# Whole-array modulation, uneven VectorE exp copies, a ring of 24 and reciprocal DMAs queued late, in an attention and GEGLU block planned by its own time model

## The chip, the cores and the metric

One core of one Trainium2 chip. The time is the device time of one execution, in microseconds (us), as a median over runs. A single core's run counts as "fast" when it is within 1.5% of the fastest run of the same kernel, otherwise "slow". Engine names in the profile: PE is TensorE (PEld its weight loads), ACT is ScalarE, DVE is VectorE, POOL is GpSimd, SP is the engine that issues the DMAs.

## The reference

```python
mod = (silu(c) @ w_mod).reshape(1, 6, 1, 512)          # sa, ca, ga, sb, cb, gb
h = layernorm(x) * (1 + ca) + sa                       # x: 2048 tokens x 512
q, k, v = h @ wqkv                                     # 32 heads of 16
p = softmax(q @ k.T / 4)                               # 32 x 2048 x 2048 exps
x = x + ga * ((p @ v) @ wo)
h = layernorm(x) * (1 + cb) + sb
out = x + gb * ((gelu(h @ w_gate) * (h @ w_up)) @ w_down)   # hidden size 1792
```

The 134 million exps are most of the work of the busiest engine (ScalarE, 842 of 902 us below). Scores are made transposed, 128 keys by 512 queries of one head at a time, so there are 32 x 16 x 4 = 2048 score tiles of 128x512.

## The kernel before

The kernel is a planner in Python: it keeps a small time model of the engines, decides by it which instruction comes next, and emits five fixed instruction streams. Every change to it, to its model as well, changes the order of everything that follows.

A score tile goes one of two ways. ScalarE exponentiates two or three at once into slots of a ring E; TensorE's PV matmuls read them and so free the slots. Or VectorE makes a "quad": it evicts four tiles, one for each of four heads, writing a linear function of the score as the bits of a bf16 number, which is a rough power of two; it then makes four copies with a constant added to the bits, and PV adds all five. Before, each copy was weighed by a V scaled to match:

```python
SHIFT = (26, 51, 77, 102)
NSL = 12            # slots of the ring E (CH = 3 per exp)
T0 = 12             # only key tiles 12 to 15 may be quads
...
v = self.vs[:, i - 1, kt - T0, :] if i else self.vaug[:, kt, :]     # scaled V for copy i
...
cand = [k for k, (u, r, g0) in enumerate(rounds)
        if u not in units[:2] and r * (512 // u[3]) >= T0]
...
if len(mem) == CH and "modB" in self.have and self.free["dve"] < t + 700:    # start or go on with a quad
```

The modulation product is a run of one-column matmuls. The helper `mm` splits any matmul of 128 rows and 128 columns of weights into four pieces of 32 columns, unless `whole` is set:

```python
def mod_cols(self, bank, base):
    for ci in range(8):
        for dc in range(NDC):            # 4
            self.mm(bank[:, ci:ci + 1], self.wmod[:, dc, base + P * ci:base + P * ci + P],
                    self.sc_bf[:, dc:dc + 1], start=(dc == 0), stop=(dc == NDC - 1))
```

At the end of a unit (one group of four heads for one set of queries) the softmax sums travel through DRAM: out, back in as 128 rows, reciprocal, out, and back broadcast. The whole chain was put into SP's queue in order:

```python
self.dma("sp", s1..., self.osb[DH:P:32, lo:hi], ...)
self.dma("sp", den, s1..., ...)
def fin1():
    self.recip(rden, den)
    self.dma("sp", s2..., rden, ...)
    for j in range(4):
        self.dma("sp", self.rb[32 * j:32 * j + 32, lo:hi], s2...broadcast_to([32, W]), ...)
...
self.task([fin1], ("den", u))
```

There are 24 units of 512 queries, then 13 of 256 and 6 of 128; QKV projections run beside the first eight, the FFN of one set of queries beside the attention of the next.

The softmax here doesn't subtract the row's maximum and nothing guards it: scores larger than these inputs give would overflow.

## Time and profile before

| | before |
|---|---|
| median of the first runs | 901.15 us (900.17 to 903.19) |
| span of the profiled run | 902.3 us |
| ScalarE busy / not busy (gaps) | 842.0 us / 60.3 us |
| VectorE busy | 687.8 us |
| VectorE evictions for quads | 188 + 92 = 280 |
| first exp | 23.59 us |

Read it from ScalarE: the span is its busy time plus the time it is not busy, its gaps. A change helps by taking work off it or by closing its gaps. The profiled run is one of the slower ones: in the rounds of the experiments the kernel before has medians of 898 to 899 us, a span of some 897, so gaps read against 60.3 us look about 6 us better than they are. Stretches of the kernel before (us; PE, PEld, DVE, ACT, POOL busy us with counts; granted TensorE clock; DMA share; GB/s):

```profile
10.00:20.00 10.00, 4.51 (x102) 2.70 (x96) 2.58 (x8) 1.55 (x2) 0.00 (x0) 0.59 1.08 363
11.90:22.10 10.20, 6.08 (x58) 2.87 (x57) 3.49 (x9) 2.24 (x3) 0.00 (x0) 0.50 1.00 348
...
90.00:100.00 10.00, 8.65 (x190) 2.48 (x186) 3.86 (x8) 6.84 (x6) 0.00 (x0) 0.69 0.03 5
93.80:104.10 10.30, 9.46 (x63) 1.69 (x62) 5.28 (x9) 6.38 (x7) 0.00 (x0) 0.50 0.09 28
95.00:100.00 5.00, 5.00 (x34) 0.89 (x33) 2.23 (x4) 2.05 (x2) 0.00 (x0) 0.50 0.03 5
```

In this profile the clock is at one half from 11.9 us, which is 1.4 us into the wait that began at 10.53, and again from 93.8 us, after the second modulation burst; each time for 10.2 us. From 95 to 100 us TensorE is busy for all of 5.00 us with only 34 matmuls while ScalarE works 2.05.

### The profile page before, as it was taken

To read this page: it belongs to the slowest core of one execution; us is meant where nothing else is said; L and a number is where in the kernel's file an instruction comes from. 1 tells how busy PE (TensorE), PEld (TensorE's weight loads), DVE (VectorE), ACT (ScalarE), POOL (GpSimd) and SP (SyncE) were. 2 spreads that over 40 slices of the span, in tenths; PEclk is the share of its full clock that TensorE was granted. 3 is DMA by queue.
4 is the path that set the end of the run, shared out by engine and by line. 5 is a ranking of instruction groups with operands and counts; after the bars stand their busy time and mean duration, and the time that the engine had idled before them with its cause. 6 is when DMAs were issued, how large, how long until landed. Compare 5 with 4: busy or idle time off the path is not lost.

```text
span 902.3 us, 28354 instructions
## 1 busy us (share of the span) xinstructions
PE 820.0 (91%) x12817; PEld 289.1 (32%) x12817; DVE 687.8 (76%) x1303; ACT 842.0 (93%) x747; POOL 3.7 (0%) x11
## 2 busy tenths in 40 slices
PE   6898999999999999999998899999988989987878
PEld 2333232322232222222222222222432333334455
DVE  5854678988899889999898899888966753735364
ACT  2999899999999999999999999999999999988882
POOL 1000000000000000000000000000000000000000
PEclk7999799999999999999999999999999999989899
DMA  9000001000002111111002211210013221544300
GB/s 303 3 26 15 15 3 26 3 27 2 26 3 83 38 49 49 49 49 38 26 2 63 74 46 49 61 39 24 27 45 113 55 84 44 153 139 125 114 10 12
DMA packets 74930, 47.68 MB, mean 53 GB/s; under 512 B 17693, under 2 KB 70618, under 8 KB 74810
## 3 DMA queue, kind: packets, MB, share of 16 engines
q1 hardware_dynamic: 72426, 44.30, 16.9%
q8 instruction: 100, 1.64, 0.8%
q10 hardware_dynamic: 2384, 1.57, 0.6%
q14 instruction: 20, 0.16, 0.1%
HBM read 43.25 MB, written 2.61 MB: 51 GB/s over the span
## 4 chain that ended last, share of the span: by engine, by line
ACT 50%; PE 32%; DVE 9%; DMA 6%; SPq 2%; issue 2%; DVEq 0%
ACT E L323 48%; PE ps_mi L310 13%; PE ps_sc L310 12%; PE ps_pv L310 6%; DMA scr_rec<-rden 2%; SPq L373 2%; DVE mreg L335 2%; ACT wreg L323 2%; DMA mreg<-in_B_w_gate_dram 1%; DMA rb<-scr_rec 1%; DVE wreg L340 1%; DVE dreg L335 1%; DVE wreg L327 1%; DMA mreg<-in_B_w_down_dram 1%; DVE wreg L344 1%
## 5 line engine op out<-in xcount | busy, mean ns | idle before, releaser
L323 ACT ACTIVATE E<-ps_sc 128x1536 bf16<-128x1536 f32 (+2 forms) x698 | 812.2, 1318 | 33.5 <-PE ps_sc L310 32.1
L310 PE MATMUL ps_sc<-qT,kmo 32*128 32x512 bf16 (+2 forms) x1408 | 184.6, 329 | 10.5 <-ACT E L323 7.5
L310 PE MATMUL ps_sc<-qT,kme 32*128 32x512 bf16 (+2 forms) x1344 | 177.9, 333 | 14.6 <-ACT E L323 12.1
L310 PE MATMUL ps_pv<-E,vaug 128*17 128x512 bf16 (+2 forms) x2380 | 176.7, 325 | 3.5 <-ACT E L323 1.7
L335 DVE TENSOR_SCALAR dreg<-ps_sc 128x512 uint16<-128x512 f32 x188 | 129.6, 690 | 37.4 <-PE ps_sc L310 35.5
L310 PE MATMUL ps_mi<-wreg,mreg 128*32 128x512 bf16 (+2 forms) x1920 | 122.9, 352 | 18.3 <-DVE wreg L340 5.6
L335 DVE TENSOR_SCALAR mreg<-dreg 128x2048 uint16<-128x2048 uint16 x188 | 123.3, 683 | 2.9 <-PE ps_pv L310 2.8
L310 PE MATMUL ps_pv<-mreg,vs 128*17 128x512 bf16 (+1 forms) x1232 | 98.4, 361 | 1.9 <-DVE mreg L335 1.4
L310 PEld LDWEIGHTS ps_sc<-qT,kme 32*128 32x128 bf16 x1344 | 46.7, 92 | 133.1 <-ACT E L323 92.0
L310 PEld LDWEIGHTS ps_sc<-qT,kmo 32*128 32x128 bf16 x1408 | 49.4, 93 | 121.7 <-ACT E L323 85.0
L310 PEld LDWEIGHTS ps_pv<-E,vaug 128*17 128x17 bf16 x2380 | 53.7, 90 | 91.8 <-issue 61.9
L335 DVE TENSOR_SCALAR mreg<-ps_sc 128x512 uint16<-128x512 f32 x92 | 63.1, 689 | 15.9 <-PE ps_sc L310 14.9
L310 PEld LDWEIGHTS ps_mi<-wreg,mreg 128*32 128x32 bf16 x1920 | 42.5, 97 | 74.1 <-issue 22.9
L335 DVE TENSOR_SCALAR mreg<-mreg 128x2048 uint16<-128x2048 uint16 x92 | 60.3, 685 | 0.9 <-PE ps_pv L310 0.8
L344 DVE CAST wreg<-ps_mi 128x512 bf16<-128x512 f32 x51 | 35.1, 688 | 23.1 <-PE ps_mi L310 22.4
L340 DVE SCALAR_TENSOR_TENSOR wreg<-wreg,ps_mi 128x512 bf16<-128x512 bf16 x51 | 34.9, 684 | 17.4 <-PE ps_mi L310 12.3
L310 PE MATMUL ps_sc<-xs,ident 128*32 128x512 bf16 (+1 forms) x349 | 31.9, 402 | 11.3 <-ACT E L323 10.7
L310 PE MATMUL ps_mi<-hreg,wreg 128*32 128x512 bf16 x480 | 40.0, 392 | 1.0 <-DVE vaug L344 0.5
L310 PEld LDWEIGHTS ps_pv<-mreg,vs 128*17 128x17 bf16 x1232 | 29.5, 89 | 34.6 <-DVE mreg L335 16.6
L327 DVE TENSOR_TENSOR onorm<-osb,rb 128x512 bf16<-128x512 f32 (+2 forms) x43 | 23.7, 550 | 21.1 <-DMA rb<-scr_rec 20.7
L310 PE MATMUL ps_mi<-mreg,hreg 128*32 128x512 bf16 x448 | 36.5, 384 | 1.2 <-DMA mreg<-in_B_w_down_dram 1.2
L310 PE MATMUL ps_mi<-wo,onorm 128*32 128x512 bf16 x480 | 36.7, 394 | 0.7 <-DVE wreg L327 0.5
(136 smaller groups left out, 563.3 us busy)
## 6 DMA issues: line engine op xcount, KB each, us to landing
mreg<-in_B_w_up_dram SPq DMA_DIRECT2D x32, 256.0 KB, 3.4
mreg<-in_B_w_gate_dram SPq DMA_DIRECT2D x28, 256.0 KB, 3.2
rb<-scr_rec SPq DMA_DIRECT2D x96, 64.0 KB, 2.0
mreg<-in_B_w_down_dram SPq DMA_DIRECT2D x16, 256.0 KB, 2.8
dreg<-in_B_w_down_dram SPq DMA_DIRECT2D x12, 256.0 KB, 4.7
mreg<-in_w_mod_dram SPq DMA_DIRECT2D x1, 2048.0 KB, 14.5
out_dram<-xs SPq DMA_DIRECT2D x16, 128.0 KB, 1.8
rb<-scr_rec SPq DMA_DIRECT2D x52, 32.0 KB, 1.8
```

The lines of the kernel that those rows point to most:

```text
L310: return self.rec("pe", lambda e: e.matmul(out, lhsT, rhs, start=start, stop=stop, tile_position=tp), [lhsT, rhs], [out], cost=(n, int(rhs ...
L323: return self.rec("act", lambda e: e.activation(out, in_, func, scale=scale, **kw), rd, wr, cost=self.cost("act", out, [in_], "act"))
L327: return self.rec(eng, lambda e: e.tensor_tensor(out, a, b, op), [a, b], [out], cost=self.cost(eng, out, [a, b], "tt"))
L335: return self.rec(eng, lambda e: e.tensor_scalar(out, a, s1, s2, **kw), rd, [out], cost=self.cost(eng, out, [a], "ts"))
L340: return self.rec("dve", lambda e: e.scalar_tensor_tensor(out, a, s, b, op0=op0, op1=op1), rd, [out], cost=self.cost("dve", out, [a, b], " ...
L344: return self.rec(eng, lambda e: e.tensor_copy(out, in_), [in_], [out], cost=self.cost(eng, out, [in_], "ts"))
L373: return e.dma_start(out, in_)
```

## The change

The intent: give VectorE more of the exps, and let TensorE run more freely. Cut to its core (left out: the SBUF layout that makes room, constants, two copy buffers for the time before modB, and the order of the key tiles, which is now plain):

```diff
-NSL = 12
+NSL = 24
-SHIFT = (26, 51, 77, 102)
-SHIFT_C = float(128 * (127 - np.log2(5) - 0.0565))
+SHIFT = (20, 43, 69, 101)
+SHIFT_C = 128 * 127 - 128 * float(np.log2(np.mean([...])))      # five copies of unlike weight
 # the time model
-            self.free[eng] = t + 50
-            self.dma_free = max(t + 1400, self.dma_free) + cost / 350
+            self.free[eng] = t + 460
+            self.dma_free = max(t + 1400, self.dma_free) + cost / 250
+            if self.fetched[0] % 128 == 0:                       # as the model assumes: one fetch per 128 matmuls
+                t = self.fetched[1] = max(t, self.fetched[1] + 3750)
+            self.fetched[0] += 1
 # modulation
+        self.whole = True
         for ci in range(8):
 # quads
-            v = self.vs[:, i - 1, kt - T0, :] if i else self.vaug[:, kt, :]
+            v = self.vaug[:, kt, :]
-        cand = [... if u not in units[:2] and r * (512 // u[3]) >= T0]
+        cand = [... if u in units[:2] or QA <= r * (512 // u[3]) < QB]          # key tiles 6 to 12
-                if len(mem) == CH and "modB" in self.have and self.free["dve"] < t + 700:
+                if len(mem) == CH and pos >= FIRST and self.free["dve"] + 600 < max(self.free["act"], t + 480) + 880 + LATE:
+                    while (self.free["dve"] + 1260 <= self.free["act"] + SLIP and self.step("dve", ...)):
+                        pass                                     # other VectorE work ahead of an eviction
 # end of a unit
-        self.task([fin1], ("den", u))
+        self.task([("sp", lambda: self.dma("sp", den, ...)), lambda: self.recip(rden, den),
+                   ("sp", lambda: self.dma("sp", s2..., rden, ...))]
+                  + [("sp", lambda j=j: rd(j)) for j in range(4)], ("den", u))
```

The last part makes each DMA a step of its own, which the planner queues when it thinks the data has landed.

More of the change, by code (lines that the diff above doesn't have):

```diff
@@ L36 @@
 SC = 2 * CH
-NSL = 12
+NSL = 24
 assert NSL % CH == 0
 LEAD = 5
-T0 = 12
 NK = 3
@@ L44 @@
 AHEAD = 24
+FIRST = 30
+AHEAD1 = 12
+LATE = 0
+SLIP = 0
+QA = 6
+QB = 13
 FLOW = 4
@@ L56 @@
 Q_SCALE = float(0.25 * np.log2(np.e) * OCT)
-SHIFT = (26, 51, 77, 102)
-SHIFT_C = float(128 * (127 - np.log2(5) - 0.0565))
+SHIFT = (20, 43, 69, 101)
+SHIFT_C = 128 * 127 - 128 * float(np.log2(np.mean([sum(
+    2.0 ** (o // 128) * (1 + (m + o) % 128 / 128) * 2.0 ** ((m + o) // 128 - o // 128) for o in (0,) + SHIFT) / 2.0 ** (m / 128)
+    for m in range(128)])))
 COMPUTE = ("pe", "act", "dve", "pool")
@@ L99, in __init__ @@
         self.whole = False
+        self.fetched = [0, 0.0]
     def sb(self, name, shape, dt):
@@ L446, in alloc @@
         self.sq = [mreg[:, 4096 + 2048 * i:6144 + 2048 * i] for i in range(NS)]
-        self.wmod = mreg[:, 0:NDC * 3072].rearrange("p (a n) -> p a n", a=NDC)
+        self.sq += [mreg[:, 2048 * i:2048 * i + 2048] for i in range(2)]
+        self.wmod = [mreg[:, 0:NDC * 1024].rearrange("p (a n) -> p a n", a=NDC),
+                     mreg[:, NDC * 1024:NDC * 3072].rearrange("p (a n) -> p a n", a=NDC)]
         dreg = sb("dreg", [P, NFC * D], BF16)
@@ L458, in alloc @@
         self.wd.append(hreg[:, NFC * 256 + 1024:NFC * 256 + 2048].rearrange("p (f n) -> p f n", f=2))
-        self.kq = [dreg[:, 0:2048], dreg[:, 2048:4096], mreg[:, 12288:14336]]
-        self.vs = sb("vs", [P, len(SHIFT), NKT - T0, H * VW], BF16)
+        self.kq = [mreg[:, 12288:14336], dreg[:, 0:2048], dreg[:, 2048:4096]]
         self.wo = sb("wo", [P, 8, D], BF16)
@@ L479, in alloc @@
         self.sc_bf = sb("sc_bf", [P, NDC], BF16)
-        self.scbc = self.onorm[:, 0, :].rearrange("p (a n) -> p a n", a=NDC)
+        self.scbc = sb("scbc", [P, NDC, P], BF16)[:, :, :]
         self.modA = sb("modA", [P, 8], FP32)
@@ L485, in alloc @@
         self.ident = sb("ident", [P, P], BF16)
-        self.ones = self.onorm[:, 1, 0:P]
+        self.ones = sb("ones", [P, P], BF16)[:, :]
         self.self32 = sb("self32", [P, P], FP32)
@@ L503, in prologue @@
         self.dma(sp, self.xs[:, 2:4, :], xv[:, 2:4, :], "x1")
-        self.dma(sp, self.wmod[:, :, 0:1024], wmv[:, :, 0:1024], "wm0")
+        self.dma(sp, self.wmod[0], wmv[:, :, 0:1024], "wm0")
         self.dma(act, self.xs[:, 4:8, :], xv[:, 4:8, :], "x2")
@@ L511, in prologue @@
             self.dma(sp, wq4[:, :, k, P:D], wqv[:, :, k, P:D], "wr%d" % k)
-        self.dma(sp, self.wmod[:, :, 1024:3072], wmv[:, :, 1024:3072], "wm1")
+        self.dma(sp, self.wmod[1], wmv[:, :, 1024:3072], "wm1")
         self.memset(dve, self.warm, 0.0)
@@ L528, in prologue @@
         for dc in range(NDC):
-            self.mm(self.scp[:, 0, dc:dc + 1], self.crow[0:1, P * dc:P * dc + P], self.onorm[0:1, 1, 0:1])
+            self.mm(self.scp[:, 0, dc:dc + 1], self.crow[0:1, P * dc:P * dc + P], self.ones[0:1, 0:1])
         self.warm_up(16)
@@ L612, in modulate, with mod_w @@
             self.ts(eng, out, in_, mod[:, 4 + dc:5 + dc], mod[:, dc:dc + 1], ALU.mult, ALU.add)
+    def mod_w(self, dc, c, n):
+        return self.wmod[0][:, dc, c:c + n] if c < 1024 else self.wmod[1][:, dc, c - 1024:c - 1024 + n]
     def mod_cols(self, bank, base):
+        self.whole = True
         for ci in range(8):
             for dc in range(NDC):
-                self.mm(bank[:, ci:ci + 1], self.wmod[:, dc, base + P * ci:base + P * ci + P],
+                self.mm(bank[:, ci:ci + 1], self.mod_w(dc, base + P * ci, P),
                         self.sc_bf[:, dc:dc + 1], start=(dc == 0), stop=(dc == NDC - 1))
+        self.whole = False
     def proj(self, bank, col, g):
@@ L702, in side_v @@
         self.done(("v", g, dc))
-        if 4 * g == T0 and not self.dry:
-            c = slice(VW * 8 * dc, VW * 8 * dc + VW * 8)
-            self.task([lambda i=i, o=o: self.ts("dve", self.vs[:, i, :, c], self.vaug[:, T0:NKT, c], float(2.0 ** (-o / 128)),
-                                                None, ALU.mult) for i, o in enumerate(SHIFT)], ("vs", dc))
         yield END
@@ L775, in side_mod @@
             for dc in range(NDC):
-                yield 512, lambda dc=dc, k=k: self.mm(mi, self.scbc[:, dc, :], self.wmod[:, dc, 512 * k:512 * k + 512],
+                yield 512, lambda dc=dc, k=k: self.mm(mi, self.scbc[:, dc, :], self.mod_w(dc, 512 * k, 512),
                                                       start=(dc == 0), stop=(dc == NDC - 1))
@@ L783, in side_mod @@
         self.done("modB")
+        if not self.dry:
+            self.sq_free.extend(range(NS))
         yield END
@@ L1018, in background @@
     def background(self, t):
+        while self.step("sp", max(self.free["sp"], t) + 40):
+            pass
         while self.free["dve"] <= t + 150 and self.step("dve", max(self.free["dve"], t) + 40):
@@ L1022, in force @@
     def force(self):
-        if not self.step("dve", None):
-            assert self.step("act", None)
+        assert any(self.step(e, None) for e in ("dve", "sp", "act"))
     def plan(self, ends, nsplit):
@@ L1128, in stream @@
             n, kpb = NKT * u[3] // 512, 512 // u[3]
-            plain = list(range(T0 // kpb))
-            m = len(plain) * 2 // 3
-            for r in plain[:m] + list(range(len(plain), n)) + plain[m:]:
+            for r in range(n):
                 add(u, r)
@@ L1150, in stream @@
         self.quad_free = list(range(NK))
-        self.sq_free = list(range(NS))
-        cand = [k for k, (u, r, g0) in enumerate(rounds)
-                if u not in units[:2] and r * (512 // u[3]) >= T0]
+        self.sq_free = [NS, NS + 1]
+        cand = [k for k, (u, r, g0) in enumerate(rounds) if u in units[:2] or QA <= r * (512 // u[3]) < QB]
         quad = None
@@ L1223, in pv_do @@
                 q["n"] -= 1
-                if i:
+                if i and (q["slots"][i] < NS or "modB" not in self.have):
                     self.sq_free.append(q["slots"].pop(i))
@@ L1261, in stream @@
                 g = None
-                if len(mem) == CH and "modB" in self.have and self.free["dve"] < t + 700:
-                    while quad is None and cand and rounds[cand[0]][2] < pos + AHEAD:
+                if len(mem) == CH and pos >= FIRST and self.free["dve"] + 600 < max(self.free["act"], t + 480) + 880 + LATE:
+                    while quad is None and cand and rounds[cand[0]][2] < pos + (AHEAD1 if rounds[cand[0]][2] < nsplit else AHEAD):
                         cand.pop(0)
@@ L1267, in stream @@
                     elif (cand and self.quad_free and (pos < ends[2] or self.credit < CREDIT) and rounds[cand[0]][2] < pos + 96 and self.backlog() < BACK
-                          and ("vs", rounds[cand[0]][0][1] // 2) in self.have
                           and all(k in self.have for k in self.keys(seq[rounds[cand[0]][2]]))):
                         rnd = rounds[cand.pop(0)]
-                        quad = {"rnd": rnd, "j": 0, "k": self.quad_free.pop(0), "ready": [], "n": NS + 1, "slots": {}}
-                        left[rnd[0]] += NS
+                        quad = {"rnd": rnd, "j": 0, "k": self.quad_free.pop(0), "ready": [], "n": 5, "slots": {}}
+                        left[rnd[0]] += 4
                         self.plain[rnd[0]] -= 1
@@ L1293, in stream @@
                     kq = self.kq[quad["k"]]
+                    while (self.free["dve"] + 1260 <= self.free["act"] + SLIP
+                           and self.step("dve", max(self.free["dve"], t) + 40)):
+                        pass
                     self.ts("dve", kq[:, 512 * j:512 * j + 512].bitcast(U16), self.scp[:, s0 + n, :], 128 / OCT, SHIFT_C,
@@ L1299, in stream @@
                         wait.append(quad)
-                        for i in range(NS):
+                        for i in range(4):
                             self.shift_task(quad, i)
@@ L1404, in unit_end, with rd @@
         self.dma("sp", s1.rearrange("(j n) -> j n", j=4), self.osb[DH:P:32, lo:hi], "da%d" % sem)
-        self.dma("sp", den, s1.rearrange("(p n) -> p n", p=P), "db%d" % sem)
-        def fin1():
-            self.recip(rden, den)
-            self.dma("sp", s2.rearrange("(p n) -> p n", p=P), rden, "dc%d" % sem)
-            for j in range(4):
-                self.dma("sp", self.rb[32 * j:32 * j + 32, lo:hi],
-                         s2[W * j:W * j + W].rearrange("(o n) -> o n", o=1).broadcast_to([32, W]), "dd%d%d" % (sem, j))
+        def rd(j):
+            self.dma("sp", self.rb[32 * j:32 * j + 32, lo:hi],
+                     s2[W * j:W * j + W].rearrange("(o n) -> o n", o=1).broadcast_to([32, W]), "dd%d%d" % (sem, j))
         def fin2():
@@ L1425, in free @@
                 ("wo", k) in self.have for k in range(sets[0]) if OCOL[k] < c + W and c < OCOL[k] + SETS[k][1])
-        self.task([fin1], ("den", u))
+        self.task([("sp", lambda: self.dma("sp", den, s1.rearrange("(p n) -> p n", p=P), "db%d" % sem)),
+                   lambda: self.recip(rden, den),
+                   ("sp", lambda: self.dma("sp", s2.rearrange("(p n) -> p n", p=P), rden, "dc%d" % sem))]
+                  + [("sp", lambda j=j: rd(j)) for j in range(4)], ("den", u))
         self.task([fin2], None, free)
@@ L1438, in tail @@
             t = self.pe_now()
-            while self.step("act", max(self.free["act"], t) + 40) or self.step("dve", max(self.free["dve"], t) + 40):
+            while any(self.step(e, max(self.free[e], t) + 40) for e in ("act", "dve", "sp")):
                 pass
```

## The prediction

> **What bounds the kernel now.** I read the page's busy shares and 40 slices first, then the table of 50 us stretches, the groups of instructions by form, the chain of waits, and the waits of the DMA-issuing queue.
>
> The page, parts 1 and 4:
>
> ```profile
> PE 820.0 (91%) x12817; PEld 289.1 (32%) x12817; DVE 687.8 (76%) x1303; ACT 842.0 (93%) x747; POOL 3.7 (0%) x11
> ...
> ACT 50%; PE 32%; DVE 9%; DMA 6%; SPq 2%; issue 2%; DVEq 0%
> ```
>
> ScalarE (ACT) is nearest to full and holds half of the chain that ended last. The stretches say where (columns: PE, PEld, DVE, ACT, POOL busy us with instruction counts, granted clock, DMA share, GB/s):
>
> ```profile
> 0.00:50.00 50.00, 37.67 (x686) 16.62 (x686) 33.47 (x107) 32.46 (x37) 3.39 (x10) 0.90 0.42 138
> 50.00:100.00 50.00, 43.83 (x849) 15.94 (x847) 23.78 (x53) 45.84 (x41) 0.31 (x1) 0.94 0.07 19
> 100.00:150.00 50.00, 45.93 (x741) 14.91 (x738) 38.79 (x65) 48.74 (x43) 0.00 (x0) 0.96 0.05 13
> ...
> 200.00:250.00 50.00, 46.27 (x513) 12.29 (x513) 44.16 (x73) 50.00 (x49) 0.00 (x0) 1.00 0.06 18
> ...
> 650.00:700.00 50.00, 43.84 (x844) 17.14 (x842) 33.51 (x72) 49.85 (x39) 0.00 (x0) 1.00 0.27 77
> ...
> 800.00:850.00 50.00, 43.09 (x1140) 24.75 (x1134) 23.41 (x53) 44.76 (x38) 0.00 (x0) 0.93 0.34 94
> ```
>
> From 150 to 750 us ACT is full, while VectorE (DVE) is idle for 11% of the middle and a third to a half of both ends. The groups show what could move between them:
>
> ```profile
> L323 ACT ACTIVATE E<-ps_sc 128x1536 bf16<-128x1536 f32 x384 | 545.2, 1510 | 18.6 <-PE ps_sc L310 17.6
> L323 ACT ACTIVATE E<-ps_sc 128x1024 bf16<-128x1024 f32 x308 | 310.6, 1094 | 6.3 <-PE ps_sc L310 5.9
> L335 DVE TENSOR_SCALAR dreg<-ps_sc 128x512 uint16<-128x512 f32 x188 | 129.6, 690 | 37.4 <-PE ps_sc L310 35.5
> L335 DVE TENSOR_SCALAR mreg<-dreg 128x2048 uint16<-128x2048 uint16 x188 | 123.3, 683 | 2.9 <-PE ps_pv L310 2.8
> L335 DVE TENSOR_SCALAR mreg<-ps_sc 128x512 uint16<-128x512 f32 x92 | 63.1, 689 | 15.9 <-PE ps_sc L310 14.9
> L335 DVE TENSOR_SCALAR mreg<-mreg 128x2048 uint16<-128x2048 uint16 x92 | 60.3, 685 | 0.9 <-PE ps_pv L310 0.8
> ```
>
> There are 2048 score tiles of 128x512. DVE takes 188+92 = 280 of them, which is 70 "quads" of four, and ACT the other 1768. A quad costs DVE four evictions at 0.69 us and four shifted copies at 0.685 us, 5.5 us in all. DVE's evictions waited 35.5+14.9 = 50 us for scores: it had room that it did not use. The mean durations of the ACT rows overlap each other, so I take ACT's price from the 200:250 stretch, where it was busy for all of 50.00 us with 17 three-tile and 32 two-tile exps, 17x1536+32x1024 = 58,880 columns: 0.85 ns a column, 0.435 us a tile. A quad therefore takes 4x0.435 = 1.74 us off ACT.
>
> The chain of waits, early (start us, us, what), and what the DMA-issuing queue waited for:
>
> ```profile
> 9.38 1.15 PE ps_sc L310 x126
> 10.53 5.49 issue
> 16.02 0.19 PE ps_sc L310 x2
> ```
>
> ```profile
> SPq L373 <- DVE osb L344: 207.3, 28, 20.0
> SPq L373 <- DVE rden L347: 162.0, 33, 17.2
> ...
> SPq L373 <- DMA scr_rec<-rden: 64.0, 39, 3.6
> SPq L373 <- DMA scr_den<-osb: 52.2, 39, 4.0
> ```
>
> TensorE (PE) stands still for 5.49 us two matmuls short of the end of the 128 one-column modulation matmuls, waiting for nothing that the profile can name. Everything up to the first exp at 23.6 us hangs on it. The queue lines show transfers held behind reciprocal DMAs whose data had not come yet; at 784 to 793 us the chain runs through six such issues and then the gate-weight load, 2.91 us, that PE needs.
>
> [...]683 ns for 2048 out of SBUF, 690 ns for only 512 out of PSUM. [...]the page's instruction queue q8 has 100 packets with 1.64 MB, and PE ran 25,634 instructions, 256 a packet. [...]I read the 5.49 us as such a crossing, because PE had run 126 small matmuls in 1.15 us and the data DMAs were moving 303 GB/s. [...]The waits above sit on the issuing queue, and rb<-scr_rec lands in 1.8 to 2.0 us. [...]Four 512-column PV matmuls span 0.39 us here, one 0.385; back to back, each further four add about 0.21 us (eight take 0.60).
>
> **The change part by part.**
> Prologue. mod_cols now issues 32 whole-array matmuls in place of 128 column pieces. 192 PE instructions go, three quarters of a block, so the crossing falls later, into the first V projection near 20 us[...]. The 32 need full-width weight loads, about 0.1 us each by the 0.097 us of the 128x128 loads in the trace, partly overlapped: 2 to 3 us from 9.35, so end near 12 in place of 16.2. Gain 4.3 us, straight on the path. The second mod_cols at 92 us has 1.00 us of the same wait: gain up to 1. Sum 5.
>
> No scaled V. The 16 vs<-vaug instructions of 294 ns go, 4.7 us of DVE between 58 and 188 us. PE's work is the same with either operand. Uneven weights cost nothing in time; their point is that any key tile may be a quad, and that nothing waits for vs.
>
> Quads. These now start at position 30 (about 35 us) instead of when modB is done (about 95 us); the first two units can have them; key tiles 6 to 12 replace 12 to 15, seven of 16 candidates in place of four; and the gate on DVE's backlog goes from "free within 0.7 us" to, roughly, "free within 0.28 us of ACT's own end", which is 1 to 1.5 us ahead. By stretch:
> - 35 to 100: DVE idle in 26 of 50 us. Only every second exp step can carry a quad tile, and the keys must be projected first. I take +4 quads. PE's projections share the bound here, so I count half of 1.74 us each: 3.5 us.
> - 100 to 650: DVE is busy 488.6 of 550 us. 269 tiles, 67 quads, are 370 us of it, the rest 119. With the time T = 550 - 1.74 n for n more quads and DVE at 0.94 busy (what I expect when half of its score waits close): 0.94 (550 - 1.74 n) = 114 + 5.5 (67.25 + n), so n = 33/7.14 = 4.6. Gain 8 us. DVE itself caps this stage: at 0.97 it would be n = 7 and 12 us.
> - 650 on: only 3 quads today, with DVE idle in 16 to 27 us of each 50. The old gate failed whenever DVE had an FFN eviction committed behind 1.08 us of matmuls; the new one passes then. But the credit test (no new quad while TensorE's side work is in arrears) stays. I take +6, at 0.8 of 1.74: 8 us.
> Sum +15 quads, 70 to 85, and 19 us.
>
> PE pays 15 quads x 4 copies x 0.21 = 13 us, in gaps[...].
>
> E ring and DMA queue. ACT waited 32.1 us for scores, of which 5.4 in 100 to 650, 3.3 in 650 to 800 and 18.0 after 800. A ring of 24 (eight groups) lets PV lag; reciprocal DMAs queued after their data lets weight loads pass. Of the 3.3 + 5 us or so that are not the tail's own serial chain I take back 4, and 2 of the 5.4: 6 us.
>
> Sum: 5 + 19 + 6 = 30 us, 901 to 871.
>
> **The rivals.** First, PE becomes the bound: around 420 to 430 us, where quads are dense, PE runs without a gap, since every change between row- and column-packed matmuls costs it some 0.1 us. Then new quads only push side work later: the middle gains 4, the end nothing, 888 us. For it: the 91%. Against: ACT waited just 5.4 us in 550. Second, DVE is saturated already, and its 50 us of score waits (0.36 us each) are too short to fill: n near 1, gain from prologue and ends only, 882. Third, the end frees up: credit turns out not to bind, DVE takes 12 or more quads after 650, and the sum is 856. Fourth, more DVE work ahead of FFN evictions lengthens the one-bank chain of matmul (1.08 us) and eviction (0.70 us) after 650 and the tail gets it back: 885. The scheduler is greedy, so a new order shifts any of this by a few us.
>
> **Range and chances.** The prologue is nearly certain; quads are the spread, 8 to 22 more. That gives 857 to 887 for 8 in 10. The 2% line is 883: below it 0.79, within 2% 0.19, slower 0.02. Slower would need TensorE to be the bound throughout, which ACT's few waits speak against.
>
> **What would show it.** First exp near 19.3 us with no issue wait over 2 us before it; no vs; ACT's score columns down by some 60 tiles, DVE's evictions near 340; DVE near 94% in the middle; quads before 95 us; ACT idle in 650 to 850 no higher. I am wrong if evictions stay under 300, or rise while ACT's waits on ps_sc rise as much (PE bound), or if the first exp does not move.

## The result, and the profile after

| | before | after |
|---|---|---|
| median | 902.17 us (900.17 to 904.77, 4 runs) | 876.72 us (870.18 to 883.59, 4 runs) |
| ratio of fast runs | | 0.9692, 95% interval 0.9629 to 0.9755 |
| span of the profiled run | 902.3 us | 875.6 us |
| ScalarE busy / not busy | 842.0 / 60.3 us | 829.2 / 46.4 us |
| VectorE busy | 687.8 us | 702.4 us |
| quad evictions | 280 | 304 |
| first exp | 23.59 us | 16.06 us |

A ratio is the mean time of one kernel's fast runs over that of the other's fast runs of the same rounds, so it isn't quite the ratio of the medians. Here it is 3.1% faster. Of the 26.7 us between the two spans, ScalarE's work gave 12.8 and its gaps 13.9.

The page of the kernel after, parts 1 and 4, which answer to the first lines of the prediction:

```profile
PE 810.4 (93%) x12637; PEld 281.9 (32%) x12637; DVE 702.4 (80%) x1335; ACT 829.2 (95%) x747; POOL 3.7 (0%) x11
...
ACT 65%; PE 20%; DVE 8%; DMA 3%; SPq 2%; issue 1%; DVEq 0%
```

ScalarE's share of the chain that ended last went from 50% to 65%: the kernel is nearer to the bound it was built for. The stretches of the kernel after:

```profile
0.00:50.00 50.00, 42.83 (x652) 17.36 (x652) 41.63 (x121) 38.98 (x45) 3.37 (x10) 0.97 0.42 138
50.00:100.00 50.00, 46.75 (x803) 16.24 (x807) 40.54 (x76) 49.80 (x48) 0.31 (x1) 1.00 0.10 24
100.00:150.00 50.00, 49.11 (x889) 17.30 (x886) 45.96 (x75) 47.28 (x43) 0.00 (x0) 1.00 0.04 8
...
200.00:250.00 50.00, 48.33 (x586) 12.93 (x588) 48.37 (x86) 50.00 (x48) 0.00 (x0) 1.00 0.06 17
...
650.00:700.00 50.00, 44.47 (x834) 17.12 (x834) 38.69 (x80) 50.00 (x42) 0.00 (x0) 1.00 0.30 82
...
800.00:850.00 50.00, 41.77 (x1295) 23.09 (x1288) 23.10 (x62) 47.02 (x37) 0.00 (x0) 1.00 0.21 59
```

Against before, the first 100 us have 10.5 us more of ScalarE at work (38.98 + 49.80 against 32.46 + 45.84) and the clock at 0.97 and 1.00 in place of 0.90 and 0.94. The groups by form:

```profile
L334 ACT ACTIVATE E<-ps_sc 128x1536 bf16<-128x1536 f32 x360 | 509.9, 1525 | 10.2 <-PE ps_sc L321 9.9
L334 ACT ACTIVATE E<-ps_sc 128x1024 bf16<-128x1024 f32 x332 | 329.2, 1125 | 4.1 <-PE ps_sc L321 3.8
...
L346 DVE TENSOR_SCALAR dreg<-ps_sc 128x512 uint16<-128x512 f32 x200 | 135.6, 686 | 13.5 <-PE ps_sc L321 12.0
L346 DVE TENSOR_SCALAR mreg<-dreg 128x2048 uint16<-128x2048 uint16 x200 | 130.9, 684 | 7.1 <-PE ps_pv L321 7.1
L346 DVE TENSOR_SCALAR mreg<-ps_sc 128x512 uint16<-128x512 f32 x104 | 70.9, 687 | 11.4 <-PE ps_sc L321 10.4
L346 DVE TENSOR_SCALAR mreg<-mreg 128x2048 uint16<-128x2048 uint16 x104 | 68.1, 686 | 7.8 <-PE ps_pv L321 7.8
```

24 three-tile exps became two-tile ones. VectorE's wait for scores fell from 50.4 to 12.0 + 10.4 = 22.4 us, but its copies now wait 7.1 + 7.8 = 14.9 us for PV to give back copy buffers, against 3.6 before. The start, from TensorE's timeline:

```profile
9.99 0.94 PE L321 MATMUL ps_sc<-sc_bf,mreg 128*128 128x1 bf16 x32 [1.32 <-DVE dreg L346]
10.86 0.61 PE L321 MATMUL ps_mi<-dreg 128*32 128x512 bf16 x8
11.41 1.07 PE L325 MATMUL ps_sc<-ident,dreg 128*128 128x128 bf16 x16
12.45 2.39 PE L321 MATMUL ps_sc<-hreg,wreg 128*32 128x512 bf16 x32
```

No wait of 5.49 us; and the 16 transposes take 1.07 us and the 32 projection matmuls 2.39, where the kernel before took 1.89 and 3.52 for them at the half clock.

A wait is still there, of 0.44 us at 16.22 us, in the V projection, and its place fits a reading. Counted through the trace (matmuls, weight loads and the sequencer's own instructions, good to one), it comes after 449 of TensorE's instructions. So do the 5.49 us of the kernel before, and the waits of experiments 2, 4, 6, 8 and 11 (5.51, 0.53, 0.54, 0.40 and 0.83 us), whatever work stands there; the second wait of the kernel before, of 1.00 us at 93.64, comes after 3009, which is 2560 or ten times 256 later. 256 is also what TensorE has per packet of the queue that the page calls `q8 instruction` (25,634 instructions before, 100 packets of 16.4 KB), and one such packet of that queue is moved from 10.53 to 16.02 us, during the 5.49 us. That fits the prediction's reading of the wait as a crossing from one block of 256 to the next; the profile itself names no cause. How long it takes, the count doesn't say. The waits of SP's queue, which answer to the last fence of the prediction:

```profile
SPq L384 <- DVE osb L355: 234.1, 29, 19.2
SPq L384 <- DVE rden L358: 141.2, 31, 16.5
...
SPq L384 <- DMA scr_rec<-rden: 31.9, 26, 2.5
SPq L384 <- DMA scr_den<-osb: 29.7, 29, 1.7
```

The waits on these DMAs, which had not landed, went from 116.2 to 61.6 us. They are not gone: the planner queues by its model, not by the chip.

Where the time came from, by stage. The bounds are the times at which VectorE copied out the 2nd, 4th, 24th and 43rd unit (85.2, 142.0, 636.2 and 878.5 us before; 73.5, 131.1, 618.1 and 847.4 after). In each stage I added the idle times of ScalarE's ACTIVATE groups, and the counts of evictions; instructions across a bound count in both stages, so the numbers are good to a tile or two. With the longer ring the exps also run further ahead of the unit that is copied out, by some 20 tiles at unit 4.

| stage | before: us, evictions, ACT idle | after: us, evictions, ACT idle |
|---|---|---|
| to unit 2 | 85.2, 0, 14.8 | 73.5, 12, 7.6 |
| to unit 4 | 56.8, 18, 4.5 | 57.5, 28, 0.1 |
| to unit 24 | 494.2, 243, 3.8 | 487.0, 244, 9.4 |
| to unit 43 | 242.4, 20, 15.0 | 229.3, 20, 3.1 |
| tail | 23.8, 0, 14.1 | 28.2, 0, 17.8 |

All the added evictions fall before unit 4 was copied out. The gaps closed at the start (11.6 us) and in the late units (11.9 us); they opened in the middle (5.6 us) and the tail (3.7 us).

### The profile page after: what moved, and what is told of

Read it like the earlier page. It is cut to its first block, busy times and chain, and to the rows that moved or that the text cites.

```text
span 875.6 us, 28031 instructions
## 1 busy us (share of the span) xinstructions
PE 810.4 (93%) x12637; PEld 281.9 (32%) x12637; DVE 702.4 (80%) x1335; ACT 829.2 (95%) x747; POOL 3.7 (0%) x11
## 3 DMA queue, kind: packets, MB, share of 16 engines
q1 hardware_dynamic: 72426, 44.30, 17.8%
## 4 chain that ended last, share of the span: by engine, by line
ACT 65%; PE 20%; DVE 8%; DMA 3%; SPq 2%; issue 1%; DVEq 0%
ACT E L334 63%; PE ps_sc L321 8%; PE ps_mi L321 7%; PE ps_pv L321 4%; SPq L384 2%; ACT wreg L334 2%; DMA rb<-scr_rec 2%; DVE mreg L346 1%; DMA scr_rec<-rden 1%; DVE dreg L346 1%; DVE kme L346 1%; DVE wreg L338 1%; DVE st L374 1%; DVE wreg L355 0%; DVE kmo L346 0%
## 5 line engine op out<-in xcount | busy, mean ns | idle before, releaser
L334 ACT ACTIVATE E<-ps_sc 128x1024 bf16<-128x1024 f32 (+2 forms) x698 | 800.1, 1326 | 23.6 <-PE ps_sc L321 23.0
L321 PE MATMUL ps_sc<-qT,kme 32*128 32x512 bf16 (+2 forms) x1344 | 179.3, 332 | 14.2 <-ACT E L334 12.2
L321 PE MATMUL ps_sc<-qT,kmo 32*128 32x512 bf16 (+2 forms) x1408 | 181.0, 329 | 11.3 <-ACT E L334 10.5
L321 PE MATMUL ps_pv<-E,vaug 128*17 128x512 bf16 (+2 forms) x2368 | 159.6, 323 | 2.0 <-issue 0.9
L346 DVE TENSOR_SCALAR dreg<-ps_sc 128x512 uint16<-128x512 f32 x200 | 135.6, 686 | 13.5 <-PE ps_sc L321 12.0
L346 DVE TENSOR_SCALAR mreg<-dreg 128x2048 uint16<-128x2048 uint16 x200 | 130.9, 684 | 7.1 <-PE ps_pv L321 7.1
L321 PE MATMUL ps_pv<-mreg,vaug 128*17 128x512 bf16 (+1 forms) x1388 | 109.0, 366 | 3.0 <-DVE mreg L346 2.4
L346 DVE TENSOR_SCALAR mreg<-ps_sc 128x512 uint16<-128x512 f32 x104 | 70.9, 687 | 11.4 <-PE ps_sc L321 10.4
L346 DVE TENSOR_SCALAR mreg<-mreg 128x2048 uint16<-128x2048 uint16 x104 | 68.1, 686 | 7.8 <-PE ps_pv L321 7.8
L321 PEld LDWEIGHTS ps_pv<-E,vaug 128*17 128x17 bf16 x2368 | 47.2, 89 | 76.9 <-issue 62.1
L351 DVE SCALAR_TENSOR_TENSOR wreg<-wreg,ps_mi 128x512 bf16<-128x512 bf16 x51 | 34.9, 685 | 14.3 <-PE ps_mi L321 10.8
L321 PEld LDWEIGHTS ps_pv<-mreg,vaug 128*17 128x17 bf16 x1388 | 33.2, 90 | 38.7 <-DVE mreg L346 19.0
L338 DVE TENSOR_TENSOR wreg<-wreg 128x1024 bf16<-128x1024 bf16 (+1 forms) x60 | 35.8, 604 | 0.7
L338 DVE TENSOR_TENSOR onorm<-osb,rb 128x512 bf16<-128x512 f32 (+2 forms) x43 | 23.5, 549 | 15.3 <-DMA rb<-scr_rec 15.2
## 6 DMA issues: line engine op xcount, KB each, us to landing
mreg<-in_w_mod_dram SPq DMA_DIRECT2D x1, 2048.0 KB, 13.9
```

Source lines behind the costliest of these rows:

```text
L321: return self.rec("pe", lambda e: e.matmul(out, lhsT, rhs, start=start, stop=stop, tile_position=tp), [lhsT, rhs], [out], cost=(n, int(rhs ...
L334: return self.rec("act", lambda e: e.activation(out, in_, func, scale=scale, **kw), rd, wr, cost=self.cost("act", out, [in_], "act"))
L338: return self.rec(eng, lambda e: e.tensor_tensor(out, a, b, op), [a, b], [out], cost=self.cost(eng, out, [a, b], "tt"))
L346: return self.rec(eng, lambda e: e.tensor_scalar(out, a, s1, s2, **kw), rd, [out], cost=self.cost(eng, out, [a], "ts"))
L351: return self.rec("dve", lambda e: e.scalar_tensor_tensor(out, a, s, b, op0=op0, op1=op1), rd, [out], cost=self.cost("dve", out, [a, b], " ...
```

## The experiments

The theory after the result: (1) the whole-array modulation gives the start, by the 5.49 us wait and by the clock; (2) the quads take work off ScalarE, but in the middle part of it is lost to gaps; (3) ring, queueing and model give the late stage. The rivals: the quads are nearly the whole gain (as the prediction had it), or the ring alone is, by letting PV lag.

**1. Whole-array modulation alone**, on the kernel before:

```diff
 def mod_cols(self, bank, base):
+    self.whole = True
     for ci in range(8):
         ...
+    self.whole = False
```

> The kernel before with one edit: the modulation matmuls issued on the whole array (32 in place of 128). My theory: the 5.49 us fetch wait goes, and with it the half-speed clock stretch after it (the kernel before ran 10.2 us cold there) and after the second such burst near 93 us (10.2 us cold). So the first exp comes at 16 to 16.5 us in place of 23.6, the cold time before 120 us falls from 20.5 us to under 7, still 280 evictions on VectorE, and the time falls by 10 to 13 us, to 889 to 892. Rival A: only the wait itself counts, 5 us or so, 897. Rival B: the stages behind are bound by something else and the head start is lost again, 900 or more.

884.18 us median (880.91 to 884.85, 6 runs) against 898.33 of before in the same rounds, ratio 0.9837 (0.9801 to 0.9873): 14 us from two lines, a little more than expected. The first exp is at 15.70 us, and 280 evictions remain. Its stretches, against those of the kernel before above (0.59 and 0.69 at the end of the same two lines there):

```profile
10.00:20.00 10.00, 8.30 (x174) 3.92 (x171) 7.65 (x27) 6.22 (x7) 0.00 (x0) 1.00 1.08 361
90.00:100.00 10.00, 9.29 (x158) 3.01 (x155) 9.13 (x15) 10.00 (x11) 0.00 (x0) 1.00 0.08 27
```

ScalarE works 6.22 and 10.00 us there, in place of 1.55 and 6.84. Its busy time over the span is nearly that of before (840.1), so the gain is gaps: 42.9 us in place of 60.3, of which 12.0 us before unit 4 was copied out. (The profile of before is a slow one; the medians differ by 14.1, the profiles by 19.3.) Both rivals fall. The edit takes away the wait and the half clock together, so it doesn't say how much is due to each.

**2. Quads alone**: the kernel after with everything else undone.

```diff
-NSL = 24
+NSL = 12
-        self.whole = True        # in mod_cols
-            self.free[eng] = t + 460 ...      # model and queueing as before
+            self.free[eng] = t + 50 ...
```

> The kernel after with everything undone but the quads (uneven weights, no scaled V, key tiles 6 to 12, early start, new gate): modulation in pieces, ring of 12, reciprocal DMAs and time model as before. 320 evictions on VectorE against 280, so 10 quads more. My theory: the first exp stays at 23.6 us with the fetch wait; the quads are worth up to 17 us by ScalarE's price, but part of it is lost to half-speed clock stretches and PE waits: time 890 to 895. Rival A (the quads are the whole gain): 880 or less. Rival B (quads are worth nothing since PE is the bound): 900 or more.

893.00 us (891.89 to 896.14, 6 runs), ratio 0.9950 (0.9916 to 0.9984): 5 us, as the theory had it. There are 40 evictions more, ScalarE's busy time fell by 17.2 us to 824.8, and its gaps rose from 60.3 to 66.6; by the medians, which differ by 5.3 us only, they rose by some 12. The wait at the start is there again (TensorE's timeline):

```profile
10.54 1.16 PE L318 MATMUL ps_sc<-sc_bf,mreg 128*32 128x1 bf16 x126 [2.43 <-DVE nwt L335]
17.20 0.19 PE L318 MATMUL ps_sc<-sc_bf,mreg 128*32 128x1 bf16 x2 [5.51 <-issue]
```

The half clock is there too, for 10.2 us, but it begins at 11.0, before the wait (11.69). The second burst, at 106.2 us and still in pieces, has neither a wait over 0.3 us nor half clock behind it.

**3. Whole-array modulation and quads**, ring of 12, old queueing and model: experiment 2 with `self.whole = True` put back.

> Both of these parts, still with a ring of 12 and the old reciprocal DMAs and time model; 320 evictions. If the two add, the time is before less the sum of what they gave alone, about 880 by my theory. What is left from there to the kernel after (about 876) is what the ring of 24, the queueing and the model give. Rival: the ring and the queueing are a major part, so that this run stays above 888.

887.23 us (885.42 to 892.47, 6 runs), ratio 0.9891 (0.9852 to 0.9930). The two do not add: this is no faster than experiment 1 with fewer evictions (0.9837), and the intervals barely overlap. So at a ring of 12 the quads were worth nothing on top. From 11.6 us it has 3.4 us of half clock, with whole-array modulation and no such wait. Something else in the change makes them pay.

**4. The kernel after once more**, unchanged, for the spread.

> The kernel after once more, for the spread of its runs: 869 to 884. My theory of that spread: [...]the time falls with the mean granted clock over the span, by about 0.85 us or a little more per 0.001: 0.988 near 868 to 870, 0.980 near 876, 0.972 near 882. Rival: time and clock are not tied within the runs of one kernel.

876.95 us (868.49 to 882.22, 6 runs), ratio 0.9719 (0.9668 to 0.9769). The four runs that came with the result had spans of 868.2, 874.1, 875.6 and 881.7 us at mean clocks of 0.988, 0.980, 0.981 and 0.972, about 0.84 us per 0.001. The profiled run here had 879.7 at 0.979, some 4 us off that line. The other five runs here lie within 2 us of the line. So clock and time go together in a run of this kernel, but what is cause and what is effect isn't settled by it. Of the half-clock stretches, those near 300, 440, 590 and 632 us are in both profiles of this kernel; one at 19 us and one at 757 us are only in the first, one at 826 us only in the second. From the first:

```profile
290.00:300.00 10.00, 7.24 (x91) 1.84 (x84) 7.99 (x14) 9.11 (x9) 0.00 (x0) 0.96 0.38 108
300.00:310.00 10.00, 10.00 (x102) 2.28 (x105) 7.30 (x12) 8.38 (x7) 0.00 (x0) 0.70 0.01 2
590.00:600.00 10.00, 10.00 (x110) 2.75 (x110) 4.11 (x7) 7.45 (x6) 0.00 (x0) 0.70 0.24 57
```

In these three stretches ScalarE misses 5.1 of 30 us. The kernel before had no such stretch in the middle.

**5. The ring of 24 put onto experiment 3.**

```diff
-NSL = 12
+NSL = 24
```

> The two parts of the third experiment (whole-array modulation, quads) with the E ring of 24 added; reciprocal DMAs and time model still as before. 316 evictions. Without the ring these two gave 887, 1.1% below before. The kernel after is some 10 us below that, and its lead arises behind 620 us, in the units of 256 and 128 queries. If the ring is what gives it: 876 to 880 here, the last score unit ending 230 to 235 us after the 24th in place of 240. If it is the queueing or the model: 884 to 889.

868.34 us (864.41 to 872.80, 6 runs), ratio 0.9666 (0.9633 to 0.9699): 19 us below experiment 3, and at least as fast as the full change. The stage was wrong, though: its last score unit still ends 240.7 us after the 24th. The ring closes gaps earlier, ScalarE's idle time from unit 2 to 24 falling from 13.9 us in experiment 3 to 2.9, and by 3.6 us in the tail. The pages' first lines, experiment 3 and then this one:

```profile
span 883.7 us, 28228 instructions
## 1 busy us (share of the span) xinstructions
PE 815.3 (92%) x12721; PEld 287.9 (33%) x12721; DVE 722.9 (82%) x1367; ACT 825.5 (93%) x748; POOL 3.7 (0%) x11
```

```profile
span 866.6 us, 27989 instructions
## 1 busy us (share of the span) xinstructions
PE 795.8 (92%) x12605; PEld 277.7 (32%) x12605; DVE 717.1 (83%) x1359; ACT 824.0 (95%) x747; POOL 3.7 (0%) x11
```

ScalarE's work is within 1.5 us of the same; its gaps are 58.2 and 42.6 us.

**6. The old queueing** in the kernel after, with ring and new model kept: `unit_end` as before.

> The kernel after with the reciprocal DMAs queued all at once at a unit's end, as before; ring of 24 and the new time model kept; 300 evictions. If queueing after the data landed gives a part of the late gain, this is 880 to 885, with waits of VectorE or TensorE on weight and reciprocal DMAs back behind 650 us (20 us in the kernel before). If it gives nothing, 873 to 879.

891.27 us (887.63 to 897.50, 6 runs), ratio 0.9920 (0.9881 to 0.9959): slower than expected, and for another reason. The late score units are not slower at all (226.4 us from unit 24 to 43), but the tail is 49.8 us in place of 28.2: FFN work was left over, and ScalarE stood 18.12 us in one piece until 862.96 us, on VectorE's GELU steps. The model now charges SP for each DMA, and with the old chain the planner builds another order. The profiled run is also 5.5 us above the median, with 20.5 us of half clock from 34.2 us and 4.6 us more of gaps to unit 2 than the kernel after. So this is a test of old queueing under the new model, not of queueing alone, and the two cannot be told apart by it.

**7. No instruction fetch in the model**, else the kernel after:

```diff
-            if self.fetched[0] % 128 == 0:
-                t = self.fetched[1] = max(t, self.fetched[1] + 3750)
-            self.fetched[0] += 1
```

> The kernel after with no instruction fetch in the planner's time model; 304 evictions, 12629 matmuls, so only the order changes. If the fetch term gives nothing, 873 to 880. If it steers the order in the stretches with many small matmuls (the units of 128 queries behind 800 us), that stretch is longer and the time 880 to 885.

871.39 us (865.14 to 880.68, 6 runs), ratio 0.9686 (0.9647 to 0.9724), within the interval of the full change (0.9692). The fetch term gives nothing that can be seen. The gaps of the middle stay as they were (9.8 us).

**8. A ring of 15** in the kernel after: `NSL = 15`.

> The kernel after with a ring of 15 in place of 24 (12 does not come through the planner's own assertion); 312 evictions. If the ring gives the late gain by letting PV lag, 880 to 886, with ScalarE waiting more for scores behind 620 us. If it does not, 873 to 879.

867.62 us (866.35 to 877.73, 6 runs), ratio 0.9672 (0.9632 to 0.9713). Fifteen slots are enough; the late stage has 2.8 us of gaps as with 24. Half-clock time between units 4 and 24 is 3.4 us here, 17.1 in the kernel after, and yet the gaps there are 7.4 against 9.4 us, one of 3.10 us standing at 178 us at full clock. So the half clock is not the whole cause of the gaps in the middle.

**9. The ring of 24 with the quad rules of before** (start after modB, key tiles 12 to 15 in their old place, old gate, no other VectorE work put ahead of an eviction; the diff is cut), unscaled V, whole-array modulation, old queueing and model:

```diff
-cand = [... if u in units[:2] or QA <= r * (512 // u[3]) < QB]
+cand = [... if u not in units[:2] and r * (512 // u[3]) >= 12]
-if len(mem) == CH and pos >= FIRST and self.free["dve"] + 600 < max(self.free["act"], t + 480) + 880 + LATE:
+if len(mem) == CH and "modB" in self.have and self.free["dve"] < t + 700:
```

> Whole-array modulation and the ring of 24, but the quads by the rules of before: only after modB, not in the first two units, only key tiles 12 to 15 in their old place, old gate, nothing put ahead of an eviction; reciprocal DMAs and time model as before. 268 evictions. By my account (ScalarE's tiles at 0.435 us each plus its idle time) this has 48 tiles more on ScalarE than the fifth experiment (316 evictions, 868 us), 21 us, and about the same idle time as that one: 886 to 890, no better than whole-array modulation alone (884). Rival, the ring alone is the gain and the quads give nothing: 866 to 873.

891.05 us (889.39 to 895.33, 6 runs), ratio 0.9928 (0.9894 to 0.9962), against 0.9837 for experiment 1. The ring alone gives nothing. With 268 evictions it has a little more work on ScalarE (843.6 us) and 45.4 us of gaps. That completes a square, all four with whole-array modulation and with old queueing and model (from three sets of rounds, in which the kernel before had 898.33, 898.06 and 899.39 us):

| | ring of 12 | ring of 24 |
|---|---|---|
| old quad rules | 884.18 (280 evictions; busy 840.1, gaps 42.9) | 891.05 (268; 843.6, 45.4) |
| new quad rules | 887.23 (320; 825.5, 58.2) | 868.34 (316; 824.0, 42.6) |

The new rules take 15 to 20 us off ScalarE in both columns. At a ring of 12 the gaps take 15.3 of it back; at 24 they don't. The planner lets a score group start only when its slots of E have been read by PV, and twelve slots are four groups; I take that limit for the reason, from the code. The runs show only that ScalarE's waits for scores grow without the slots.

**10. The new queueing under the old model**, ring of 24, quads, whole-array modulation.

```diff
-            self.free[eng] = t + 460
-            self.dma_free = max(t + 1400, self.dma_free) + cost / 250
+            self.free[eng] = t + 50
+            self.dma_free = max(t + 1400, self.dma_free) + cost / 350
```

(and no fetch term).

> Whole-array modulation, quads, ring of 24 and the new queueing of the reciprocal DMAs, with the whole time model as before; 312 evictions. If the queueing alone takes away the late waits on weight transfers (TensorE waited 9.0 us for gate weights between 620 and 800 us in the fifth experiment, ScalarE 9.4 us for scores), ScalarE's idle time there falls to 3 us or less and the time is 860 to 866. If it is the time model that does it, or both are needed, 868 to 873.

875.03 us (874.56 to 879.92, 6 runs), ratio 0.9750 (0.9720 to 0.9781): slower than without the new queueing (0.9666). ScalarE's late gaps were 11.4 us, not 3. TensorE's waits on weight transfers fell all the same, from 9.0, 2.5 and 1.1 us in experiment 5 to 1.8, 0.8 and 0.2 (620 to 860 us). So late queueing shortens these waits, as it was meant to, but that did not close ScalarE's late gaps (13.4 us in experiment 5), and VectorE waited longer for the reciprocals (18.9 us in place of 10.8). With the new DMA costs even the old queueing leaves TensorE 0.3 us of waits for weights (experiment 6). The late gaps are small only where the model's DMA costs are new as well (after: 3.1, experiment 6: none, experiment 7: 1.6, experiment 8: 2.8). TensorE's waits for weights in the kernel after, in the same stretch:

```profile
PE ps_mi L321 <- DMA mreg<-in_B_w_gate_dram: 0.4, 1, 0.4
PE ps_mi L321 <- DMA mreg<-in_B_w_down_dram: 0.4, 1, 0.4
PE ps_mi L321 <- DMA mreg<-in_B_w_up_dram: 0.3, 1, 0.3
```

**11. Modulation in pieces again**, in experiment 5: without `self.whole = True`.

> The fifth experiment (868 us) with the modulation matmuls in 128 pieces again; 316 evictions. If what the whole-array form gives adds to the rest as it stood alone (14 us), 880 to 884, first exp near 23.6 us and the clock at half for 7 to 10 us after it. If the larger ring makes up for a late start, 870 to 875.

875.26 us (871.89 to 876.89, 5 runs), ratio 0.9734 (0.9703 to 0.9766): 7 us above experiment 5, at the edge of the second expectation. In its profiled run the wait at the same place was short:

```profile
12.74 0.19 PE L318 MATMUL ps_sc<-sc_bf,mreg 128*32 128x1 bf16 x2 [0.83 <-issue]
```

The first exp came at 19.68 us. Half clock lasts 6.8 us there, from 10.8, again before the wait (11.91), and none follows the second burst. So the wait has 5.49, 5.51 and 0.83 us in three profiled runs, and the worth of the whole-array form is 7 to 14 us by what stands around it.

**12. A version meant to beat both**: experiment 8 with the gate 60 ns wider (`LATE = 60`).

> A version meant to be faster than both: the kernel after with a ring of 15 (868 in the eighth experiment, with no long half-speed stretch in the middle) and a gate 60 ns wider for the quads: 316 evictions in place of 312. By my account 4 tiles fewer on ScalarE are 1.7 us: 865 to 868 if its idle time stays at the eighth experiment's 32 us. The order changes everywhere, so that the idle time may differ by 5 us either way; above 873 would mean that the account does not carry from one schedule to the next to within a per cent.

873.52 us (871.11 to 874.68, 6 runs), ratio 0.9716 (0.9686 to 0.9745): a miss. ScalarE's busy time fell by 1.8 us to 823.4 as the account has it, and its gaps rose from 39.9 to 49.5, 12.2 of them in the middle and 17.6 in the tail. Work carries from one schedule to the next; gaps don't. A gate 60 ns wider, which costs nothing in itself, moved the time by 6 us with intervals that just overlap: differences of 6 to 7 us between two orders of this planner, as in experiments 9 (against 1), 10 and 11 (against 5), can't be put down to the edited part with certainty. The 19 us of the ring under the new rules, and the 14 us of experiment 1, are well above that. The fastest kernels stay experiments 5 and 8, at 868 us; their intervals overlap with that of the full change, so I call them not slower rather than faster.

## Why the prediction was right, and where it was wrong

The time (871 predicted, 876.72 measured, 857 to 887 the range) and the direction were right, and so was the bound: ScalarE's work and its gaps. The sum was right with terms that were not, too small at the start and too large for the quads, so that it came out near is in part luck.

- **Prologue, 5 us.** The wait went as the prediction read it; the size was wrong. Alone it gave 14 us (experiment 1), and 7 with all else in place (experiment 11). The wait that it read as the crossing did fall into the V projection, as foreseen, 0.44 us at 16.22 us. Two things were missed. The 32 full-width loads with their matmuls took 0.94 us, not 2 to 3. And TensorE ran at half clock from 11.9 us, which cost 2.0 us in transposes and projections before the first exp, and from 93.8 us, where experiment 1 closed 4.2 us of gaps between units 2 and 4. The first exp came at 16.06, not 19.3. The clock's records of the kernels before and after hold two values, 0.50 (as from 95 to 100 us) and 1.00, and the half-clock stretches last 10.2, 6.8 or 3.4 us. What sets the clock is not shown. The clock column of the prediction's own stretches had 0.90 and 0.94 in it, and I read past them.
- **No scaled V, 4.7 us of VectorE.** It was left as no gain in itself. No run tests it alone.
- **Quads, 15 more and 19 us.** 6 more (304 evictions). Early: 22 evictions, 5.5 quads, against 4. From 100 to 650: 4.6 predicted, 0 found (243 and 244 evictions to unit 24). The step that failed is "DVE at 0.94 busy (what I expect when half of its score waits close)": the waits did close, from 50.4 to 22.4 us, and VectorE's busy share from 100 to 600 us rose only from 444.58 to 458.92 of 500 us (92%), the copies now waiting for PV. On the count in the middle the second rival came out right, but not for its reason: VectorE was not full. With 15 slots the same rules place 257 evictions there, and by time, from 100 to 650 us (before, after, experiment 8):

```profile
100.00:650.00 550.00, 520.14 (x6784) 154.64 (x6781) 488.62 (x832) 544.42 (x492) 0.00 (x0) 1.00 0.12 35
100.00:650.00 550.00, 522.93 (x6983) 154.31 (x6983) 490.97 (x851) 539.78 (x489) 0.00 (x0) 0.98 0.13 36
100.00:650.00 550.00, 521.20 (x7133) 155.86 (x7125) 509.94 (x891) 541.04 (x494) 0.00 (x0) 1.00 0.13 36
```

  In those 550 us 265, 265 and 276 evictions start. Experiments 3 and 5 have 284 and 276, which is 4.75 and 2.75 quads more than before, with VectorE at 514.75 and 511.85 us or 0.94 and 0.93: the prediction's figures for this stretch were nearly met there, and not in the kernel after. The number of quads is the planner's, fixed by its model when the kernel is built, and the prediction worked it out from VectorE's idle time on the chip; that step failed. (It counts 269 evictions in this stretch before; the views have 177 + 88 = 265, which leaves its result as it is.) From 650 on: 6 predicted, 0 found. ScalarE's busy time fell by 12.8 us, of which 24 tiles at the prediction's 0.435 us are 10.4.
- **E ring and queueing, 6 us, as a term of their own.** This step had the wrong form. The ring is not a term: with the old rules it gives nothing, and without it the new rules give nothing (the square in experiment 9). It belongs in the condition of the quads. The late gaps fell by 11.9 us; I had put 4 there, by way of weight loads that are let pass. That way failed: experiment 10 has those waits at 2.8 in place of 12.6 us and late gaps of 11.4 against 13.4. The gaps close with the model's new DMA costs. In time, queueing and model together gave nothing on top of ring, quads and whole-array form (0.9666 in experiment 5, 0.9692 in the kernel after).
- **What was not foreseen.** Gaps of 5.6 us more in the middle and 3.7 in the tail. Half-clock stretches go with part of them (in the kernel after, 5.1 of the 9.4 us); experiments 8 and 12 have 7.4 and 12.2 us of gaps in the middle with 3.4 us of half clock, so the cause of the rest stays open.
- **Rivals.** TensorE as the bound fell: its records are busy 810.4 us, and ScalarE waited for scores 23.0 us in place of 32.1. In the middle, from 100 to 650 us, it waited more, 9.6 in place of 5.4, with no more quads there. The change between row- and column-packed matmuls, which the first rival prices at 0.1 us, shows from 420 to 430 us in the kernel before: groups of four 512-column matmuls start 0.32 us apart where the packing changes and 0.22 us where it does not. The fourth rival, a longer tail, came true by 4.4 us (23.8 to 28.2), though not by VectorE's quads, of which the tail has none.

## What to carry to other kernels

Split the span of a kernel with one bound engine into that engine's work and its gaps: the work of a change can be priced beforehand, the gaps of a planned order cannot. Test two parts that share a buffer together as well as alone; here more quads and a longer ring were each worth nothing or less, and 16 us together. And read the clock column first: here a burst of 128 tiny matmuls met a wait of 5.49 us, which I read as a block crossing, and the half clock around it (10.2 us) cost time of its own, which the prediction left out.

## What the runs leave open

- The wait at the start was 5.49, 5.51 and 0.83 us at the same instruction in three profiled runs (338 GB/s on the DMA queues during the first of them); the kernel after, with a quarter of those matmuls, had 0.44 us, later, in the V projection. What makes it long or short stays open: the 126 small matmuls in 1.15 us that the prediction names ran before the short one too (1.16 us in experiment 11). It came after 449 of TensorE's instructions in all seven profiles that have it, and the next one was seen 2560 later, which fits blocks of 256.
- How a burst of one-column matmuls, or the wait, bears on the clock stays open. In the first 25 us half clock lasts 10.2, 10.2 and 6.8 us in the three profiles with the burst in pieces (kernel before, experiments 2 and 11), and none or 3.4 us in the eleven with the whole-array form. The wait is not shown to be the cause: in experiments 2 and 11 half clock began before it, and experiment 3 has 3.4 us without it.
- A single load of 128x128 in the burst shows 95 ns in the trace of the kernel after, but 32 of them with one-column matmuls took 0.94 us, 29 ns each. The time of one load is thus not what this row of loads cost.
